# A fused mLSTM, MoE and cosine-MLP kernel: expert steps, exponentials and weight loads placed anew around the last attention chunks

## The chip, the cores and the metric

The kernel runs on one core of a Trainium2 chip. The metric is device time in microseconds (us) from one launch to its end. TensorE is called PE here, VectorE DVE, ScalarE ACT, GpSimd POOL and SyncE SP, as in the profile. Each engine works through its own instructions strictly in order, and waits on semaphores for the others.

## The reference

Three layers follow each other in float32. The first is an mLSTM over 2 batches, 8 heads, 768 positions and head size 40. The second is a mixture of 8 experts with top-2 routing, and the third is an MLP with x·cos(x) between its two products.

```
C = f_stab * C + i_stab * outer(v_t, k_t); n = f_stab * n + i_stab * k_t
y_t = sigmoid(o_t) * (C q_t) / max(|n q_t|, 1)
...
logits = x @ w_gate;  noise_scale = log1p(exp(x @ w_noise))
top2 of logits + noise_scale * noise, softmax over the two
out[mask] += top2_w[mask, k] * (relu(x[mask] @ w1[e]) @ w2[e])
...
h = x @ w_in;  out = (h * cos(h)) @ w_out
```

## The kernel before

The recurrence is computed in chunks of 128 positions, 6 for each batch, so there are 12 chunks, 0 to 11. `att_step(n)` writes the instructions of chunk n. For PE these are `mm_state(n)` (L274, the chunk's contribution to the state), the products `mm_s(n + 2)` (L256, queries by keys of the chunk after next), `mm_out(n)` (L314 and L318, four pairs of heads into one PSUM tile), the transposes `rt_a(n - 1)` (L354) and the router's product `rt_b(n - 1)` (L363). `mm_out(n)` calls `between(w)` after each of its four head pairs w, and other PE work can be put there. ACT makes the decay factors `mk_e(n + 1)` (L230, tile `get`), the exponentials of the weights `mk_w` (L210, eight instructions, tile `wt`; POOL then masks them, L217), the copy `xTt` of the transposes (L356), the copy `Lt` of the router's product (L367) and the absolute value `Abs` (L329) with which `mk_y(n)` begins. DVE adds the state (`mk_state`, L301), multiplies the weights in (`mk_p`, L264), forms the scaled queries (`mk_q`, L244, on POOL for some n) and ends `mk_y(n)` with L335, which makes the chunk's output rows `x(n)`. POOL also scales the keys (L236) and decays the state (`mk_decay`, L285).

When chunk 5 is done, the first batch can be routed. `router_a0` to `router_a4`, `router_b`, `router_b1`, `router_b2`, `router_c` and `router_d` rank its tokens; `router_c` (L511, twelve small matmuls, the index product) and `router_d` (L519, L520) give the rows that POOL then gathers (`gather`, L552, an indirect DMA into `xgt`). `router_s` (L482 to L484) prepares the second batch's offsets. `prep_slot` transposes gathered rows (L561), ACT copies them to `xh` (L563) and DVE forms the rest `xl` (L564, L566).

The experts come in ten groups of eight steps, 80 steps in all. Experts 0 and 1 form a small group for each batch, so that groups 0 and 1 (steps 0 to 15) need the first batch alone; groups 2 to 7 need both. `expert_step` first splits the weights two steps ahead (`split(k + 2)`: ACT copies to `wh`, L591, then DVE or POOL forms the rest `wl`, L593), then writes the first product (L600, eight matmuls), relu on ACT (L652) and the rest on DVE (L655), and then the second product (L605, L606, L609) of the step before it. `POOL_SPLIT` and a list of even numbers decide which splits go to DVE and which to POOL.

The order is written by hand. `at[n]`, `pre[n]`, `mid[n]` and `fill[n]` are lists of calls that `att_step(n)`, and later the loop over expert steps, writes at four places: `pre` behind `mk_e`, `mid` behind `mm_out`, `fill` behind the loads, `at` behind the whole chunk or step. Steps 0 to 3 stand in chunks 10 and 11, step 4 behind the last chunk, and the loop goes on with `K0 = 5`. SP issues all other transfers in the written order; `load_w` (L538) brings expert weights into two large buffers `wraw`. The PSUM tile `pM` exists once, `pS` three times and `pA` four times; who takes a tile waits until its last reader is done. Two places are to be followed in the code:

```
elif w == NH - 2 and n != 10:
    rt_a(n - 1, psS if n == 7 else None)
...
pre[9] = [(mk_w, (11, False))]
mid[9] = [(router_c, (0,)), (router_d, (0,)), (gather, (0, 0)), (gather, (0, 1)), (mk_m, (11, 0, 1)), (split, (0,))]
mid[10] = [(mk_y, (10,)), (rt_a, (9,)), (prep_slot, (0, 0, psA)), (prep_slot, (0, 1, psA))]
fill[10] = [(step, (0,))]
```

Of the kernel before, what the change touches and what calls it, by code (L numbers as in the profile page):

```python
# [41 lines left out]
def tile_mlstm_moe_moe2(ctx, tc, qk, kv, og, gi, gf, wcat, noise, wm1, wm2, cst, out):  # L42
# [539 lines left out]
    POOL_SPLIT = (1, 7, 9, 11, 65, 67, 75)  # L582

    def split(k):
        g, f = divmod(k, 8)
# [274 lines left out]
    def att_step(n):  # L860
# [51 lines left out]
        if n == 10:  # L912

            for p, r0, st, m in ((64, ROW0[2] + CAP2, 512, 6), (16, CAP1, 256, 2), (16, ROW1[0] + CAP1, 256, 2)):
                Y.dma_start(bass.AP(tensor=YD.tensor, offset=YD.offset + r0 * DM, ap=[[DM, p], [st * DM, m], [1, DM]]),
                            cc_[:p, None, 0:DM].to_broadcast([p, m, DM]))
# [25 lines left out]
    mid[9] = [(router_c, (0,)), (router_d, (0,)), (gather, (0, 0)), (gather, (0, 1)), (mk_m, (11, 0, 1)), (split, (0,))]
    fill[9] = [(split, (1,))]
    put(9, router_a3, 0)
    put(10, router_a4, 0)
    mid[10] = [(mk_y, (10,)), (rt_a, (9,)), (prep_slot, (0, 0, psA)), (prep_slot, (0, 1, psA))]
    fill[10] = [(step, (0,))]
    put(10, step, 1)
    mid[11] = [(mk_y, (11,)), (step, (2,))]
    put(11, step, 3)  # L950
# [19 lines left out]
    put(6, router_b, 1)  # L970
    put(7, router_b1, 1, 0)
    put(7, router_b1, 1, 1)
    put(8, router_b2, 1)
    put(9, router_p, 1)
    put(10, router_c, 1)
    put(10, router_d, 1)
    put(11, router_a3, 1)
    put(12, router_a4, 1)
# [194 lines left out]
```

## Time and profile before

| what | us |
|---|---|
| median of 3 runs | 516.35 |
| lowest and highest of them | 514.23, 517.95 |
| the profiled execution's own time | 515.04 |
| its span in the profile | 513.2 |
| PE busy in that span | 485.0 |
| DVE, ACT, POOL busy | 365.9, 326.0, 273.4 |

The span goes from the first to the last instruction; 1.84 us lie around it. PE is busy for 95% of it, so time is lost or won where PE waits. Chunks 6 to 11 and the first expert steps, which the change touches, lie between 53 and 127 us. A start and a duration of overlapping matmuls are modelled, so starts are compared with starts.

### The profile page before, as it was taken

To read this page: it belongs to the slowest core of one execution; us is meant where nothing else is said; L and a number is where in the kernel's file an instruction comes from. 1 tells how busy PE (TensorE), PEld (TensorE's weight loads), DVE (VectorE), ACT (ScalarE), POOL (GpSimd) and SP (SyncE) were. 2 spreads that over 40 slices of the span, in tenths; PEclk is the share of its full clock that TensorE was granted. 3 is DMA by queue.
4 is the path that set the end of the run, shared out by engine and by line. 5 is a ranking of instruction groups with operands and counts; after the bars stand their busy time and mean duration, and the time that the engine had idled before them with its cause. 6 is when DMAs were issued, how large, how long until landed. Compare 5 with 4: busy or idle time off the path is not lost.

```text
span 513.2 us, 9200 instructions
## 1 busy us (share of the span) xinstructions
PE 485.0 (95%) x3294; PEld 470.0 (92%) x3294; DVE 365.9 (71%) x776; ACT 326.0 (64%) x695; POOL 273.4 (53%) x234
## 2 busy tenths in 40 slices
PE   4998996999999999999999989899999999999994
PEld 3998996899999999999999988899999999999994
DVE  8875596687388777777775688698856665787772
ACT  3668865466455554555454566578877777787772
POOL 5435576476856777676867686273365347200000
PEclk9999999999999999999999999999999999999998
DMA  5778866782755646282939183220021003001001
GB/s 167 241 244 266 246 217 220 207 325 84 279 187 187 241 166 263 82 347 59 372 94 323 56 335 108 80 66 15 0 78 39 2 14 96 8 2 38 1 2 44
DMA packets 25397, 74.41 MB, mean 145 GB/s; under 512 B 3872, under 2 KB 11392, under 8 KB 25344
## 3 DMA queue, kind: packets, MB, share of 16 engines
q1 hardware_dynamic: 22752, 65.14, 36.9%
q0 software_dynamic: 2592, 8.61, 5.5%
q8 instruction: 28, 0.46, 0.4%
q14 instruction: 25, 0.20, 0.1%
HBM read 64.51 MB, written 9.22 MB: 144 GB/s over the span
## 4 chain that ended last, share of the span: by engine, by line
PE 79%; DVE 9%; ACT 6%; issue 2%; DMA 2%; SPq 0%; DVEq 0%; ACTq 0%
PE pS L600 35%; PE pA L609 11%; PE pA L606 10%; PE pA L605 10%; ACT wt L210 2%; PE pM L561 2%; PE pS L318 2%; PE pA L256 2%; PE pA L618 1%; PE pA L617 1%; DMA gb<-gd 1%; PE pM L363 1%; DVE c_t L723 1%; ACT get L230 1%; PE pS L314 1%
## 5 line engine op out<-in xcount | busy, mean ns | idle before, releaser
L593 POOL TENSOR_TENSOR wl<-wraw,wh 128x704 fp32r<-128x704 f32 x69 | 122.7, 1787 | 59.4 <-ACT wh L591 52.2
L655 DVE SCALAR_TENSOR_TENSOR hb<-pS,hb 128x384 fp32r<-128x384 f32 (+2 forms) x128 | 45.9, 390 | 45.2 <-ACT hb L652 44.6
L591 ACT ACTIVATE wh<-wraw 128x704 fp32r<-128x704 f32 x80 | 62.9, 786 | 14.2 <-PE pA L617 7.5
L600 PE MATMUL pS<-xh,wh 128*128 128x448 f32 (+1 forms) x240 | 69.5, 344 | 0.5 <-ACT xh L563 0.5
L600 PE MATMUL pS<-xh,w 128*128 128x384 f32 x288 | 66.5, 340 | 1.6 <-DVE m_t L764 1.5
L600 PE MATMUL pS<-xh,wl 128*128 128x448 f32 (+1 forms) x240 | 65.7, 328 | 0.3 <-POOL wl L593 0.3
L606 PE MATMUL pA<-wl,hb 128*128 128x320 f32 x208 | 62.1, 308 | 0.0
L605 PE MATMUL pA<-wh,hb 128*128 128x320 f32 x208 | 62.1, 308 | 0.0
L749 ACT ACTIVATE m_t<-pS,magic 128x384 f32<-128x384 f32 x64 | 37.0, 579 | 27.9 <-PE pS L600 24.7
L652 ACT ACTIVATE hb<-pS 128x448 fp32r<-128x448 f32 (+1 forms) x80 | 37.7, 471 | 26.1 <-PE pS L600 17.2
L600 PEld LDWEIGHTS pS<-xh,w 128*128 128x128 f32 x288 | 49.8, 188 | 2.9 <-DVE m_t L764 2.9
L764 DVE SCALAR_TENSOR_TENSOR m_t<-m_t,pS 128x384 f32<-128x384 f32 x64 | 35.4, 553 | 16.8 <-ACT m_t L763 14.7
L609 PE MATMUL pA<-wh,hb 128*128 128x320 f32 x208 | 44.0, 310 | 3.1 <-DVE hb L655 3.0
L600 PEld LDWEIGHTS pS<-xh,wl 128*128 128x128 f32 x240 | 42.7, 188 | 2.8 <-POOL wl L593 0.5
L750 DVE TENSOR_SCALAR m_t<-m_t 128x384 f32<-128x384 f32 x64 | 23.1, 361 | 26.6 <-ACT m_t L749 26.4
L600 PEld LDWEIGHTS pS<-xh,wh 128*128 128x128 f32 x240 | 40.4, 189 | 1.6 <-ACT xh L563 0.6
L770 POOL TENSOR_TENSOR wl<-m_t,wh 128x384 fp32r<-128x384 f32 x25 | 25.4, 1017 | 30.4 <-ACT wh L768 21.2
L600 PE MATMUL pS<-xl,wh 128*128 128x448 f32 (+1 forms) x160 | 39.6, 329 | 0.6 <-DVE xl L564 0.6
L605 PEld LDWEIGHTS pA<-wh,hb 128*128 128x128 f32 x208 | 38.7, 186 | 0.8
L606 PEld LDWEIGHTS pA<-wl,hb 128*128 128x128 f32 x208 | 38.6, 186 | 0.6
L552 POOL DMA_INDIRECT xgt<-xd,idx x28 | 34.5, 1230 | 7.0 <-issue 3.0
L751 DVE SCALAR_TENSOR_TENSOR m_t<-pS,m_t 128x384 f32<-128x384 f32 x64 | 35.7, 558 | 2.2
(198 smaller groups left out, 1239.7 us busy)
## 6 DMA issues: line engine op xcount, KB each, us to landing
wraw<-wm SPq DMA_DIRECT2D x36, 704.0 KB
raw<-wm SPq DMA_DIRECT2D x16, 704.0 KB
gb<-gd SPq DMA_DIRECT2D x10, 512.0 KB
kv<-kv SPq DMA_DIRECT2D x12, 324.0 KB
qk<-qk SPq DMA_DIRECT2D x24, 160.0 KB
yd<-yt SPq DMA_DIRECT2D x22, 160.0 KB
wraw<-wm SPq DMA_DIRECT2D x8, 352.0 KB
ogt<-og SPq DMA_DIRECT2D x6, 320.0 KB
```

Source lines behind the costliest of these rows:

```text
L552: G.indirect_dma_start(out=t[:n, :], out_offset=None, in_=XD[0:S, :] if g < 2 else XD[:, :], in_offset=bass.IndirectOffsetOnAxis(ap=(idxe ...
L591: A.activation(wh, raw[:, f, :], AF.Copy)
L593: eng.tensor_tensor(out=wl, in0=raw[:, f, :], in1=wh.bitcast(FT), op=OP.subtract)
L600: T.matmul(p[:, :n], w[:, 128 * k:128 * k + 128], x[:, m, :], start=(i == 0), stop=(i == 7))
L605: T.matmul(a[:n, :DM], hh[:, s], wh[:, KW:], start=first, stop=False)
L606: T.matmul(a[:n, :DM], hh[:, s], wl[:, KW:], start=False, stop=False)
L609: T.matmul(a[:n, :DM], hl[:, s], wh[:, KW:], start=False, stop=last)
L652: A.activation(hh[:, :n], p[:, :n], AF.Relu)
L655: V.scalar_tensor_tensor(out=hb[:, o:o + z - a], in0=p[:, a:z], scalar=0.0, in1=hh[:, a:z].bitcast(FT), op0=OP.max, op1=OP.subtract)
L749: A.activation(t, m["p"], AF.Identity, bias=magic, scale=0.5 / PI)
L751: V.scalar_tensor_tensor(out=t, in0=m["p"], scalar=0.5 / PI, in1=t, op0=OP.mult, op1=OP.subtract)
L764: V.scalar_tensor_tensor(out=s, in0=s, scalar=1.0, in1=m["p"], op0=OP.subtract, op1=OP.mult)
```

## The change

No arithmetic is added or removed. Steps 0 to 3 leave chunks 10 and 11: only step 0's first product still stands in chunk 11, behind its outputs, step 1 comes behind the last chunk, and the loop starts with `K0 = 2`. The index product, its conversion and the first two gathers move from the place behind all of chunk 9's outputs to that behind its first pair of heads. The exponentials of chunks 9 and 10 move from the ends of chunks 7 and 8 to the beginnings of chunks 7 and 8 (as those of chunk 11 already stood at the beginning of chunk 9). The ACT table load moves from the middle of chunk 6 to the end of chunk 5. `rt_a(8)` takes a `pS` tile and `rt_b(8)` the `pM` tile, `rt_a(9)` stands between the heads of chunk 10, and `mk_y(10)` behind chunk 10's fill. The splits, weight loads, the clearing of `yd`, the second batch's router and the gathers of group 2 get other steps, and four splits and one `mk_q` change their engine.

```diff
-        (G if n in (1, 4, 5, 6, 7, 8, 9, 11) else V).tensor_tensor(out=d["qt"], in0=d["qk"][:, 1], in1=d["ge"], op=OP.mult)
+        (G if n in (1, 4, 5, 6, 7, 8, 9) else V).tensor_tensor(out=d["qt"], in0=d["qk"][:, 1], in1=d["ge"], op=OP.mult)
...
-    POOL_SPLIT = (1, 7, 9, 11, 65, 67, 75)
+    POOL_SPLIT = (1, 3, 7, 65, 67, 75)
...
-            elif w == NH - 2 and n != 10:
-                rt_a(n - 1, psS if n == 7 else None)
+            elif w == NH - 2:
+                rt_a(n - 1, psS if n in (7, 9) else None)
+            if w == 0 and n == 9:
+                router_c(0)
+                router_d(0)
+                gather(0, 0)
+                gather(0, 1)
...
-        if n < 9:
+        if n < 7:
             mk_w(n + 2)
...
-        put((6, 7, 8, 8, 8, 9, 9, 9)[i], load_w, 0, i, 1)
+        put((6, 7, 7, 8, 10, 10, 10, 11)[i], load_w, 0, i, 1)
...
-    mid[6] = [(A.preload_act_table_set, ("natural_log_exp_and_others",))]
+    put(NC - 1, A.preload_act_table_set, "natural_log_exp_and_others")
...
+    pre[7] = [(mk_w, (9,))]
+    pre[8] = [(mk_w, (10,))]
...
+    fill[10] = [(split, (0,)), (split, (1,))]
+    put(10, router_a3, 0)
+    put(10, prep_slot, 0, 0, psA)
+    mid[11] = [(mk_y, (11,)), (prep_slot, (0, 1, psA))]
+    fill[11] = [(step, (0,))]
...
+        put(11, gather, 1, i)
-    K0 = 5
+    K0 = 2
...
-    step(4)
+    step(1)
```

Three places show how the engines' instructions stand. The first is ACT from the end of chunk 5 (the tanh, L158) to chunk 7, before:

```order
L158 ACTIVATE ogt<-ogt 128x640
L230 ACTIVATE get<-gb 64x512 x2
L356 ACTIVATE xTt<-pM 128x384
L881 ACT_TABLE_LOAD
L367 ACTIVATE Lt<-pM 128x16
...
L210 ACTIVATE wt<-gb,tok 128x128 x8
L230 ACTIVATE get<-gb 64x512 x2
L356 ACTIVATE xTt<-pS 128x384
L367 ACTIVATE Lt<-pM 128x16
```

The same stretch of the change:

```order
L158 ACTIVATE ogt<-ogt 128x640
L960 ACT_TABLE_LOAD
L230 ACTIVATE get<-gb 64x512 x2
L356 ACTIVATE xTt<-pM 128x384
L367 ACTIVATE Lt<-pM 128x16
...
L210 ACTIVATE wt<-gb,tok 128x128 x8
L230 ACTIVATE get<-gb 64x512 x2
L210 ACTIVATE wt<-gb,tok 128x128 x8
L356 ACTIVATE xTt<-pS 128x384
L367 ACTIVATE Lt<-pM 128x16
```

The table load now stands ahead of `mk_e(7)` and the copy `xTt(5)`, and the eight exponentials of chunk 9 ahead of the copy `xTt(6)`. The second place is PE in chunk 9, the change as a difference with its - and +. L511 is the index product, of whose twelve weight loads and matmuls the first row ends the piece; L354 are the transposes `rt_a(8)`.

```order
 L256 MATMUL pA<-qk_93 128x128 x2
-L314 MATMUL pS<-st_99,qtt 128x82
-L318 MATMUL pS<-kv,ppt 128x2x41 x2
-L256 MATMUL pA<-qk_93 128x128 x2
-L314 MATMUL pS<-st_99,qtt 128x82
-L318 MATMUL pS<-kv,ppt 128x2x41 x2
-L354 MATMUL pM<-ident,xt 128x128 x3
-L314 MATMUL pS<-st_99,qtt 128x82
-L318 MATMUL pS<-kv,ppt 128x2x41
-L318 MATMUL pS<-kv,ppt 128x82
-L256 MATMUL pA<-qk_93 128x128 x2
 L511 LDWEIGHTS r_am
```

Three pairs of heads and the transposes of chunk 8, which stood ahead of the index product, stand behind it now. The third place is ACT from the factors `mk_e(11)` in chunk 10 to the first relu, before:

```order
L230 ACTIVATE get<-gb 64x512 x2
L329 ACTIVATE pS<-pS 128x8
L356 ACTIVATE xTt<-pM 128x384
L563 ACTIVATE xh<-pA 128x3x128
L563 ACTIVATE xh<-pA 128x3x112
L367 ACTIVATE Lt<-pM 128x16
L591 ACTIVATE wh<-wraw 128x704
L652 ACTIVATE hb<-pS 128x240
```

And there in the change:

```order
L230 ACTIVATE get<-gb 64x512 x2
L356 ACTIVATE xTt<-pM 128x384
L367 ACTIVATE Lt<-pM 128x16
L591 ACTIVATE wh<-wraw 128x704 x2
L329 ACTIVATE pS<-pS 128x8
L436 ACTIVATE r_w_1147<-r_w_1147 128x6
L563 ACTIVATE xh<-pA 128x3x128
L356 ACTIVATE xTt<-pM 128x384
L329 ACTIVATE pS<-pS 128x8
L563 ACTIVATE xh<-pA 128x3x112
L367 ACTIVATE Lt<-pM 128x16
```

Two weight copies L591 stand ahead of `Abs(10)` (the first L329), and the exponential L436 of `router_a3` ahead of the copies that follow.

## Rows read from the trace of the kernel before

**Rows 1.** The page's part 1: busy us, share of the span, instructions

```profile
PE 485.0 (95%) x3294; PEld 470.0 (92%) x3294; DVE 365.9 (71%) x776; ACT 326.0 (64%) x695; POOL 273.4 (53%) x234
```

**Rows 2.** PE's timeline, chunk 6 to step 5: start, us, instruction, [idle before, releaser]

```profile
58.60 0.94 PE L363 MATMUL pM<-wc,xTt 128*128 128x128 f32 x6 [0.38 <-ACT xTt L356]
...
65.43 0.91 PE L363 MATMUL pM<-wc,xTt 128*128 128x128 f32 x6 [0.39 <-DVE r_os L429]
...
75.36 0.35 PE L314 MATMUL pS<-st,qtt 128*128 128x82 f32 x2
...
80.03 0.45 PE L511 MATMUL pM<-r_bm,r_am 128*128 128x32 f16 x12 [1.31 <-ACT xTt L356]
...
83.34 0.45 PE L314 MATMUL pS<-st,qtt 128*128 128x82 f32 x2 [0.85 <-DVE qtt L244]
...
86.09 0.49 PE L354 MATMUL pM<-ident,xt 128*128 128x128 f32 x3
...
88.72 0.94 PE L363 MATMUL pM<-wc,xTt 128*128 128x128 f32 x6 [1.53 <-ACT xTt L356]
...
90.78 0.49 PE L600 MATMUL pS<-xl,wh 128*128 128x240 f32 x2 [0.62 <-DVE xl L564]
...
93.43 0.56 PE L609 MATMUL pA<-wh,hb 128*128 128x320 f32 x2 [0.37 <-DVE hb L655]
...
101.26 0.47 PE L600 MATMUL pS<-xh,wh 128*128 128x240 f32 x2
...
103.11 0.83 PE L363 MATMUL pM<-wc,xTt 128*128 128x128 f32 x6
103.70 0.47 PE L600 MATMUL pS<-xh,wh 128*128 128x240 f32 x2
```

**Rows 3.** ACT's timeline, chunk 6 to step 5

```profile
58.05 0.49 ACT L356 ACTIVATE xTt<-pM 128x384 f32<-128x384 f32 x1
58.56 1.28 ACT L881 ACT_TABLE_LOAD   x1
...
59.86 0.18 ACT L367 ACTIVATE Lt<-pM 128x16 f32<-128x16 f32 x1
...
64.33 0.49 ACT L356 ACTIVATE xTt<-pS 128x384 f32<-128x384 f32 x1
...
77.16 2.44 ACT L210 ACTIVATE wt<-gb,tok 128x128 f32<-128x128 f32 x8
79.51 0.46 ACT L356 ACTIVATE xTt<-pM 128x384 f32<-128x384 f32 x1
79.88 0.78 ACT L591 ACTIVATE wh<-wraw 128x704 fp32r<-128x704 f32 x1
...
88.00 0.15 ACT L329 ACTIVATE pS<-pS 128x8 f32<-128x8 f32 x1
...
103.98 0.18 ACT L367 ACTIVATE Lt<-pM 128x16 f32<-128x16 f32 x1 [1.01 <-PE pM L363]
```

**Rows 4.** DVE's timeline, chunk 8 to step 12

```profile
74.72 0.56 DVE L502 TENSOR_TENSOR r_bm<-r_jm,tok_id 128x384 f16<-128x384 f32 x1
...
84.58 2.11 DVE L435 TENSOR_TENSOR r_w<-r_mx 128x6 f32<-128x6 f32 x1
...
89.17 0.49 DVE L335 SCALAR_TENSOR_TENSOR xt<-pS,ogt 128x320 f32<-128x320 f32 x1
...
118.21 0.16 DVE L435 TENSOR_TENSOR r_w<-r_mx 128x6 f32<-128x6 f32 x1
```

**Rows 5.** POOL's timeline, chunks 9 and 10

```profile
82.42 0.94 POOL L552 DMA_INDIRECT xgt<-xd,idxe  x1 [0.31 <-issue]
...
84.56 1.68 POOL L593 TENSOR_TENSOR wl<-wraw,wh 128x704 fp32r<-128x704 f32 x1
86.19 1.01 POOL L285 TENSOR_TENSOR st<-st,get 40x164 f32<-40x164 f32 x2
```

**Rows 6.** Tile xgt over the whole run: time of the gathers to landing

```profile
DMA to landing us min/median/max: 2.9/5.2/5.6
```

More of the change, by code (lines that the diff above doesn't have):

```diff
@@ L591, in split @@
         A.activation(wh, raw[:, f, :], AF.Copy)
-        eng = V if len(groups[g][1]) == 2 and (k % 2 and k not in POOL_SPLIT or k in (12, 14)) else G
+        eng = V if len(groups[g][1]) == 2 and (k % 2 and k not in POOL_SPLIT or k in (10, 12)) else G
         eng.tensor_tensor(out=wl, in0=raw[:, f, :], in1=wh.bitcast(FT), op=OP.subtract)
@@ L911, in att_step, with clear_yd @@
             gates_b(4, NC)
[L912 to L916, printed above, removed]
+    def clear_yd():
+        for p, r0, st, m in ((64, ROW0[2] + CAP2, 512, 6), (16, CAP1, 256, 2), (16, ROW1[0] + CAP1, 256, 2)):
+            Y.dma_start(bass.AP(tensor=YD.tensor, offset=YD.offset + r0 * DM, ap=[[DM, p], [st * DM, m], [1, DM]]),
+                        cc_[:p, None, 0:DM].to_broadcast([p, m, DM]))
     at, pre, mid, fill = {}, {}, {}, {}
@@ L928, in tile_mlstm_moe_moe2 @@
     for i in range(8):
-        put((6, 7, 8, 8, 8, 9, 9, 9)[i], load_w, 0, i, 1)
-    put(10, load_w, 1, 0, 2)
-    put(11, load_w, 1, 2, 2)
-    put(11, load_w, 1, 4, 2)
-    mid[6] = [(A.preload_act_table_set, ("natural_log_exp_and_others",))]
+        put((6, 7, 7, 8, 10, 10, 10, 11)[i], load_w, 0, i, 1)
+    put(11, load_w, 1, 0, 2)
+    put(NC - 1, A.preload_act_table_set, "natural_log_exp_and_others")
     fill[6] = [(router_a0, (0,))]
@@ L936, in tile_mlstm_moe_moe2 @@
     put(6, router_a2, 0)
+    pre[7] = [(mk_w, (9,))]
     fill[7] = [(router_b, (0,))]
     put(7, router_b1, 0, 0)
+    pre[8] = [(mk_w, (10,))]
     fill[8] = [(router_b1, (0, 1)), (router_b2, (0,))]
-    put(8, router_s)
     pre[9] = [(mk_w, (11, False))]
[L942 to L950, printed above, removed]
+    fill[9] = [(mk_m, (11, 0, 1))]
+    put(9, router_s)
+    fill[10] = [(split, (0,)), (split, (1,))]
[3 more added lines that the diff above has]
+    fill[11] = [(step, (0,))]
+    put(11, router_a4, 0)
     for i in range(2):
-        put(9, gather, 1, i)
-    K0 = 5
+        put(11, gather, 1, i)
+    K0 = 2
     for n in range(2 * NC):
@@ L964, in tile_mlstm_moe_moe2 @@
     wp = ctx.enter_context(tc.tile_pool(name="wp", bufs=1, reuse_waits="tile"))
-    put(5, load_w, 1, 6, 2)
-    put(5, router_a2, 1)
+    put(2, load_w, 1, 2, 2)
+    put(2, clear_yd)
+    put(3, load_w, 1, 4, 2)
+    put(4, load_w, 1, 6, 2)
+    put(3, router_a2, 1)
+    put(4, router_b, 1)
+    put(5, router_b1, 1, 0)
     put(5, prep_slot, 1, 0, psA)
+    put(6, router_b1, 1, 1)
     put(6, prep_slot, 1, 1, psA)
[L970 to L978, printed above, removed]
+    put(7, router_b2, 1)
+    put(8, router_p, 1)
+    put(8, router_c, 1)
+    put(8, router_d, 1)
+    put(10, router_a3, 1)
+    put(11, router_a4, 1)
     for i in range(4):
-        put(10 + i // 2, gather, 2, i)
+        put(8 + i // 2, gather, 2, i)
         put((13, 14, 15, 15)[i], prep_slot, 2, i, (psA, psM)[i % 2])
@@ L988, in tile_mlstm_moe_moe2 @@
         for h in range(4):
-            put(9 + 8 * i + 2 * h if i else (6, 6, 7, 7)[h], load_w, e, 2 * h, 2)
+            put(9 + 8 * i + 2 * h if i else 9 + h, load_w, e, 2 * h, 2)
     def conv_sched(f, ks):
```

4 lines of the change are left out of this document (2 added, 2 removed).

## The prediction

> **What bounds the kernel now.** I read the page's busy times first. PE is busy 485.0 us [rows 1] of a span of 513.2, and the edits leave PE's list of work as it is, so the change can only move PE's waits. The second view is PE's timeline from chunk 6 to step 5 [rows 2]: the reader is to look at the brackets, where a wait and its releaser stand. Seven rows have one, of 0.38, 0.39, 1.31, 0.85, 1.53, 0.62 and 0.37 us: 5.45 us, which is about all that can be won here. Third, for each of them, the timelines of ACT [rows 3], DVE [rows 4] and POOL [rows 5], where one sees what the late engine did instead. At 80.03 PE has no work of its own that is late: the index product needs the tile `pM`, which is free when `xTt(8)` is copied, and ACT does chunk 11's exponentials first, from 77.16 to 79.51. At 83.34 chunk 10's outputs wait for DVE, at 88.72 the router's product waits for a copy on ACT, which had waited for a DVE subtraction of six columns that took 2.11 us [rows 4]. So this stretch is bound by the chain ACT, DVE, POOL between chunks, with expert steps as filler between them.
>
> I follow one clock, the start of the same piece of PE work in both kernels, and call the difference the delay.
>
> **Chunk 6: the table load goes ahead.** ACT is at work without a gap when it copies `xTt(5)` at 58.05; right behind it comes the table load of 1.28 us, and `Lt(5)` starts at 59.86 [rows 3]. PE's router product waits for that copy [rows 2]. The load holds ACT from the copy's end, 58.54, to its own, 59.84. With it ahead of `mk_e(7)` and the copy, these come 1.30 later, and so does PE: delay +1.30. Before, the load lay beside PE's next products and cost PE nothing. A bound from below is zero, if ACT had slack there, which its gapless row speaks against. The Trainium skill (page ScalarE: Activation LUTs, section What ACT_TABLE_LOAD costs) puts the load at 1283 ns and, with a drain, every switch to another set at about 2.66 us. By that figure the estimate of this term would be 2.66, and the total 1.36 above the sum below. The trace agrees with the 1283 ns and shows no drain: the load begins 0.02 us after the copy's end, and `Lt(5)` starts 0.02 us after the load's.
>
> **Chunk 7: chunk 9's exponentials go ahead of xTt(6).** `Lt(5)` needs the router's product, 0.87 us from its start (103.11 to 103.98 [rows 2, 3]), so it starts at 59.90 + 0.87, about 60.8. From `Lt(5)` to `xTt(6)` ACT needs 4.47 us (59.86 to 64.33, no gap [rows 3]); eight exponentials are added, 2.35 (77.16 to 79.51). `xTt(6)` so starts at 67.6, ends at 68.1, and PE's product starts at 68.15 instead of 65.43 [rows 2]: delay +2.72, 1.42 of it from this step. The other waiter there, DVE's ranking, is only 0.9 later and done before. Everything of chunk 8 then runs at +2.72 without a wait, since ACT has the exponentials of chunk 9 behind it.
>
> **Chunk 9: the index product.** It now stands behind the first pair of heads, where PE begins the second pair at 75.36 [rows 2]; with the delay that is 78.1. Its last input `r_bm` ended at 75.28 [rows 4], with the delay 78.0. So it starts at once or a few tenths late; I add 0.2. `rt_a(8)` in a `pS` tile is copied before PE needs it, since chunk 11's exponentials end earlier than it starts. The waits of 1.31 and 0.85 go, and PE runs on from there: three pairs, the transposes and the router's product (0.6, 103.11 to 103.70) bring chunk 10's heads to 83.0 instead of 83.34 [rows 2]. Delay there -0.3.
>
> **Chunks 10 and 11, the filler taken out.** Heads to transposes take 2.75 (83.34 to 86.09 [rows 2]), about 0.68 a pair. `rt_a(9)` stands behind the third pair, its copy is done at 86.1, when the fourth pair ends: the wait of 1.53 goes. Then new waits come, because there is nothing left to put between:
> - `Lt(9)` is at 86.1 + 0.87 = 87.0. Two weight copies of 0.78 [rows 3] stand between it and `Abs(10)`, so that is at 88.5, and x(10) is ready 1.66 later (88.00 to the end of L335, 89.66 [rows 3, 4]), at 90.2. Chunk 11's heads start at 87.1; after three pairs, at 89.1, `rt_a(10)` waits for x(10): 1.1 us.
> - `r_w` L435 follows x(10) on DVE. It took 0.16 us at one place and 2.11 at another, where it ended at 86.69, in the middle of POOL's state decay, whose two halves follow a split of 1.68 [rows 4, 5]. So it waits for a POOL operation. Now POOL does two splits from 88.0 to 91.4, and L435 ends there, not at 90.4. I take the upper value, since the splits lie over it. Queued behind it are the exponential L436, `xh` and `xTt(10)` on ACT; `xTt(10)` ends at 92.5, PE is free at 91.55: 1.0 us.
> - `xl` of the second slot stands on DVE behind `mk_y(11)`, which needs `Abs(11)`, behind `xTt(10)`: ready at 94.65. PE has then done four of step 0's eight matmuls and waits 0.9 (before 0.62 [rows 2]).
> - Step 0's first product ends at 95.2; transposes 0.3, step 1's first product 1.0, step 0's second 0.9, router 0.6: step 2 begins at 98.0.
>
> Before, the step behind the last router product (step 5) begins at 103.70, with three more steps done; a step takes 1.85 (101.26 to 103.11 [rows 2]). 103.70 - 3 x 1.85 = 98.15. So the delay at step 2 is **-0.15**, and +0.05 with the 0.2 of chunk 9. The gains of chunks 9 and 10 pay for the losses of chunks 6, 7 and 11.
>
> **Gathers.** The decay of the state for chunk 11 waits on POOL for the landing of the first two gathers. The first starts about 79.8, the second 81.2, and landing takes 2.9 to 5.6 [rows 6]: the second lands between 84.1 and 86.8. Mask, weights and queries of chunk 11 follow it on POOL and DVE, so the heads start between 87.1 and 89.9. Up to 89.2 that is covered by the wait for x(10); beyond it costs up to 0.7. `router_s`, behind `mk_y(9)` on DVE now, lies under the same cover.
>
> **Steps 2 to 16.** The second batch's chain gets three more steps in front of step 16, but PE prepares the last slot right ahead of step 16 in both orders and waits for its copy, so nothing is won there. POOL gets split 3 and two gathers of 0.94 [rows 5] behind split 2: with splits of 1.70, split 3 is ready at 100.0, and step 3 wants it at 100.15; up to 1.0 if one of them slips. DVE takes splits 9, 10 and 11 instead, in steps 7 to 9, where its ranking is lighter. Weight loads: split 4's transfer is issued behind x(10)'s store, at about 91, and wanted at 99; each later one has as long. I cost these at zero; their cover is those 8 us. From step 16 on both orders are the same.
>
> **Sum.** 515.04 (the profiled execution) + 1.30 + 1.42 + 0.2 - 2.87 (what chunks 9 to 11 give back net) = 515.1. The profiled execution lies 1.31 below the median of the three runs, so against that: 516.35 + 0.05, **516.4 us**. Ends of the unknown costs: table term 0 to 1.30, L435 0 to 1.0, index product 0 to 0.7, gathers 0 to 0.7, POOL behind step 0 0 to 1.0. All low: 516.4 - 1.3 - 1.0 - 0.2 = 513.9; all high: 516.4 + 0.5 + 0.7 + 1.0 = 518.6.
>
> **Rivals.**
> - Gain: ACT's later copies don't reach PE, so that chunks 6 and 7 cost nothing and chunks 9 to 11 give back what I count. For it: the exponentials are only moved, and their burst in chunk 9 goes. Against it: ACT's gapless rows from 58.05 to 64.33. The time is 516.4 - 2.72 = 513.7; with none of the three waits of chunk 11 either, 510.9.
> - Slower: POOL becomes the bound behind the attention. In steps 0 to 4 it does splits 0 to 4, 1.7 each, and two gathers, and DVE's operations on SBUF and POOL's hold each other up, as L435 beside a split shows [rows 4, 5]. If split 2 slips past 97, each step from 3 to 5 waits for its `wl`, about 1 us a step: 519.4; with late gathers 520.1. It decides from the point where split 3 ends after 100.2.
> - The loads: two buffers are filled later than before, and a step that waits for one waits whole transfers. If split 4 or 5 waits, 3 to 5 us: about 520. Against it: some 8 us of lead.
> - The table load holds ACT twice as long, since ACT has to run empty first: once more 1.30, 517.7. The load's neighbours at 0.02 us speak against it [rows 3]. This is the drain of the page named above.
>
> **How the numbers follow.** Forecast (514.6 to 518.2): 0.60. Gain: 0.20, mostly 511.3 to 514.6. POOL-bound: 0.12, loads: 0.05, both 518.2 to 522. Longer load: 0.03. The range 513.0 to 519.4 leaves out about 0.09 below and 0.08 above. About 1% (5.2 us) is what a measurement of this kernel can tell from no change. Faster by more (below 511.2) is only the far end of the gain, 0.05; slower by more (above 521.5) the far end of the late transfers and POOL, 0.06; within it 0.89.
>
> **What the profile after would show.** Chunk 6: `xTt(5)` right behind `mk_e(7)` and the load, PE's bracket at the router's product about 1.7. Chunk 7: `xTt(6)` behind eight exponentials, a bracket of about 1.8. Chunk 9: no bracket at L511 over 0.5, none at L314 of chunk 10. Chunk 11: a bracket at L354 for x(10) near 1.1, one at L363 near 1.0 with L435 longer than 1 us on DVE, one at L600 near 0.9. Step 3: no bracket for `wl`. The prediction is wrong if the brackets of chunks 6 and 7 are missing (gain), or if steps 2 to 5 show waits for `wl` or a weight load (loss).

## The result, and the profile after

The changed kernel took 519.96 us (median of 21 runs, 517.49 to 523.81), the kernel before 514.87 (21 runs, 513.65 to 518.89). The ratio is 1.0095, with an interval of 1.0075 to 1.0115: 4.9 us slower, by 3.9 to 5.9. The prediction was 516.4, with a range up to 519.4. It forecast a change of +0.05 on a base of 516.35, the median of three runs; over 21 runs the kernel before is at 514.87. So the base was 1.5 too high, by chance in the direction of the result: the two times lie 3.6 apart, but the error in the change itself is 4.9. The profiled execution of the changed kernel took 517.49, the fastest of the 21, with a span of 515.7; that of the kernel before took 515.04, with a span of 513.2. So two things have to be explained: 2.5 us between two profiles, and about 2.5 more between the profile of the changed kernel and its own median.

The busy times, which answer to [rows 1]:

```profile
PE 486.9 (94%) x3294; PEld 471.9 (92%) x3294; DVE 366.2 (71%) x778; ACT 326.3 (63%) x695; POOL 270.9 (53%) x232
```

PE has the same 3294 matmuls as before, and yet 1.9 us more busy time. Work that didn't change has become slower somewhere. PE's timeline, which answers to [rows 2] (start, us, instruction, idle before and releaser):

```profile
59.29 0.94 PE L363 MATMUL pM<-wc,xTt 128*128 128x128 f32 x6 [1.44 <-ACT xTt L356]
...
67.61 0.94 PE L363 MATMUL pM<-wc,xTt 128*128 128x128 f32 x6 [1.88 <-DVE ppt L264]
...
77.57 0.45 PE L511 MATMUL pM<-r_bm,r_am 128*128 128x32 f16 x12
...
87.56 0.45 PE L314 MATMUL pS<-st,qtt 128*128 128x82 f32 x2 [0.62 <-DVE qtt L244]
...
90.03 0.52 PE L354 MATMUL pM<-ident,xt 128*128 128x128 f32 x3 [0.24 <-DVE xt L335]
...
92.12 0.94 PE L363 MATMUL pM<-wc,xTt 128*128 128x128 f32 x6 [0.65 <-ACT xTt L356]
...
94.30 0.49 PE L600 MATMUL pS<-xl,wh 128*128 128x240 f32 x2 [0.80 <-DVE xl L564]
...
97.63 0.47 PE L600 MATMUL pS<-xh,wh 128*128 128x240 f32 x2
...
111.27 0.45 PE L609 MATMUL pA<-wh,hb 128*128 128x320 f32 x2
113.61 0.46 PE L511 MATMUL pM<-r_bm,r_am 128*128 128x32 f16 x12 [1.90 <-DVE r_fl L476]
```

The reader sees the waits of chunks 6 and 7, the index product of chunk 9 without one, the waits of chunk 11 (0.62 for `qtt`, then 0.24, 0.65 and 0.80), and step 2 beginning at 97.63. All these stand in the prediction, with other sizes in chunk 11. The row of chunk 7 names DVE's `ppt`, which ends at 67.61. What the product reads is the copy `xTt`, which ends at 67.56 on ACT:

```profile
64.74 2.44 ACT L210 ACTIVATE wt<-gb,tok 128x128 f32<-128x128 f32 x8
67.09 0.47 ACT L356 ACTIVATE xTt<-pS 128x384 f32<-128x384 f32 x1
```

The last row of PE's timeline does not stand in the prediction: in step 8 the second batch's index product waits 1.90 us for the tile `pM`, whose old content `r_fl` still reads. Before, this product stood behind step 10 and had no wait:

```profile
115.85 0.47 PE L511 MATMUL pM<-r_bm,r_am 128*128 128x32 f16 x12
```

DVE's timeline of the changed kernel shows why `r_fl` is late:

```profile
109.50 0.90 DVE L593 TENSOR_TENSOR wl<-wraw,wh 128x704 fp32r<-128x704 f32 x1
110.42 0.41 DVE L655 SCALAR_TENSOR_TENSOR hb<-pS,hb 128x240 fp32r<-128x240 f32 x1
110.75 0.56 DVE L500 TENSOR_TENSOR pM<-pM,cc 128x384 f32<-128x384 f32 x1
111.34 0.56 DVE L502 TENSOR_TENSOR r_bm<-pM,tok_id 128x384 f16<-128x384 f32 x1
111.81 0.88 DVE L593 TENSOR_TENSOR wl<-wraw,wh 128x704 fp32r<-128x704 f32 x1
112.61 0.40 DVE L655 SCALAR_TENSOR_TENSOR hb<-pS,hb 128x240 fp32r<-128x240 f32 x1
112.93 0.48 DVE L630 COPY yt<-pA 112x320 f32<-112x320 f32 x1
113.33 0.16 DVE L474 TENSOR_SCALAR r_pos<-pM 128x12 uint32<-128x12 f32 x1
113.40 0.15 DVE L476 TENSOR_TENSOR r_fl<-pM,cc 128x8 f32<-128x8 f32 x1
```

No row has a bracket: DVE never waits here. Two of its rows are the splits 9 and 10 (`wl`, 0.90 and 0.88), which the change gave to DVE. (Five splits changed their engine, not four: 3 and 14 went to POOL, and 9, 10 and 11 to DVE.) They stand ahead of the ranking's last operations, and POOL has nothing to do from 109.07 to 114.79. The index product's own input `r_bm` is ready at 111.90, 1.7 us before the product starts. The windows of the same stretch (PE, PEld, DVE, ACT, POOL busy, granted clock of PE, DMA share, GB/s):

```profile
110.00:112.00 2.00, 1.72 (x14) 1.45 (x12) 1.94 (x5) 1.55 (x4) 0.00 (x0) 1.00 0.05 8
112.00:114.00 2.00, 0.39 (x13) 0.39 (x13) 1.72 (x6) 0.73 (x2) 0.00 (x0) 1.00 0.24 81
114.00:116.00 2.00, 2.00 (x14) 2.00 (x11) 1.17 (x3) 0.29 (x1) 1.21 (x1) 0.56 0.76 186
116.00:118.00 2.00, 2.00 (x11) 2.00 (x11) 0.41 (x1) 0.71 (x2) 1.39 (x3) 0.58 0.95 352
118.00:120.00 2.00, 2.00 (x18) 2.00 (x18) 1.29 (x3) 1.01 (x4) 1.56 (x2) 1.00 1.04 430
```

Right behind the wait the granted clock goes from 1.00 to 0.50 (2.4 to 1.2 GHz) for 3.4 us, with PE busy throughout. At half clock, 3.4 us do the work of 1.7: that is most of PE's additional busy time of 1.9. Everything behind is later by the wait and by this stretch.

### The profile page after: what moved, and what is told of

Same layout as the page of the kernel before. It is cut to its first block, busy times and chain, and to the rows that moved or that the text cites. A ratio compares the mean times of both kernels' runs of the same rounds, so it can differ in the third digit from the quotient of the medians.

```text
span 515.7 us, 9208 instructions
## 1 busy us (share of the span) xinstructions
PE 486.9 (94%) x3294; PEld 471.9 (92%) x3294; DVE 366.2 (71%) x778; ACT 326.3 (63%) x695; POOL 270.9 (53%) x232
## 4 chain that ended last, share of the span: by engine, by line
PE 75%; DVE 7%; ACT 2%; issue 2%; POOL 1%; DVEq 0%; ACTq 0%; POOLq 0%
PE pS L600 35%; PE pA L609 10%; PE pA L606 10%; PE pA L605 10%; PE pM L561 2%; PE pA L618 1%; PE pA L617 1%; PE pS L318 1%; DVE c_t L723 1%; PE pA L256 1%; PE pM L363 1%; ACT xh L563 1%; DVE m_t L764 1%; DVE c_t L727 1%; DVE wl L593 0%
## 5 line engine op out<-in xcount | busy, mean ns | idle before, releaser
L593 POOL TENSOR_TENSOR wl<-wraw,wh 128x704 fp32r<-128x704 f32 x68 | 121.0, 1790 | 61.6 <-ACT wh L591 52.5
L591 ACT ACTIVATE wh<-wraw 128x704 fp32r<-128x704 f32 x80 | 62.8, 786 | 15.3 <-PE pA L617 9.1
L600 PE MATMUL pS<-xh,wh 128*128 128x448 f32 (+1 forms) x240 | 69.8, 345 | 0.5 <-ACT xh L563 0.5
L600 PE MATMUL pS<-xh,w 128*128 128x384 f32 x288 | 66.5, 340 | 1.6 <-DVE m_t L764 1.5
L600 PE MATMUL pS<-xh,wl 128*128 128x448 f32 (+1 forms) x240 | 66.3, 330 | 0.4 <-POOL wl L593 0.4
L600 PEld LDWEIGHTS pS<-xh,w 128*128 128x128 f32 x288 | 49.8, 188 | 2.9 <-DVE m_t L764 2.9
L609 PE MATMUL pA<-wh,hb 128*128 128x320 f32 x208 | 44.1, 311 | 2.8 <-DVE hb L655 2.6
L600 PEld LDWEIGHTS pS<-xh,wl 128*128 128x128 f32 x240 | 43.1, 190 | 3.1 <-POOL wl L593 0.8
L600 PEld LDWEIGHTS pS<-xh,wh 128*128 128x128 f32 x240 | 40.9, 190 | 1.6 <-ACT xh L563 0.6
L600 PE MATMUL pS<-xl,wh 128*128 128x448 f32 (+1 forms) x160 | 39.8, 330 | 0.8 <-DVE xl L564 0.8
```

Of the source, the lines that this page charges most:

```text
L600: T.matmul(p[:, :n], w[:, 128 * k:128 * k + 128], x[:, m, :], start=(i == 0), stop=(i == 7))
L609: T.matmul(a[:n, :DM], hl[:, s], wh[:, KW:], start=False, stop=last)
```

## More profiles, and a table of them

The theory after the first profile: the loss is the wait of step 8, and the stretches at half clock that follow it and the waits of chunks 6 and 7 in some executions. Its rival: each wait costs its own length and no more, and what else differs between executions is something else. A profile is one execution. Three more of the changed kernel and one of the kernel before were taken, with no edit.

> The changed kernel as it is, a second profile, to see whether the places at which the granted clock falls are the same in every execution. By the clock theory (a wait of PE of 1.4 us or more is followed by a stretch at half clock in some executions and not in others) the instructions are the same but the stretches are not: a fall is to be expected behind the L511 wait of step 8 (1.9 us, about +1.6), and now also one in chunk 6 or 7, where the first profile had waits of 1.44 and 1.88 us at clock 1.00; span 515.7 to 519. By the rival, that the loss is waits alone, the profile repeats the first: span 515.7, clock below 1.00 only at 114 to 118.

> The changed kernel once more, a third profile. Two profiles had the same waits (1.9 us in chunk 7, 1.9 us at step 8) but one stretch at half clock each: behind step 8 in the first (span 515.7), behind chunk 7 in the second (517.8). If the clock falls behind each of these waits by chance, this profile has one or both (about 1.5 us for step 8, 3.0 for chunk 7), and its span is 514.2 + 0.7 for the start + the falls: 516 to 519.5. If the spread of the times has another cause, a span of 517 or more comes with the clock at 1.00 throughout.

> The changed kernel, a fourth profile, with the same expectation as the third: the span follows the half-clock stretches behind the waits of chunk 7 (3.0) and step 8 (1.5); or, by the rival, it varies with the clock at 1.00.

> The kernel before, a second profile: by the clock theory it has no half-clock stretch between chunk 6 and step 16, since its longest wait there is 1.5 us and has filler work around it; span 513 to 514. If such stretches are there as often as in the changed kernel, the clock doesn't tell the two kernels apart.

The spans were 517.8, 515.5 and 514.8 (times 519.53, 517.20, 516.52), and 513.0 for the kernel before (514.85). The second profile of the changed kernel has the same wait in chunk 7 as the first, and the same in step 8:

```profile
68.51 0.94 PE L363 MATMUL pM<-wc,xTt 128*128 128x128 f32 x6 [1.87 <-DVE ppt L264]
...
72.72 1.06 PE L318 MATMUL pS<-kv,ppt 128*128 128x82 f32 x4
...
76.63 0.61 PE L318 MATMUL pS<-kv,ppt 128*128 128x82 f32 x4
...
117.54 0.46 PE L511 MATMUL pM<-r_bm,r_am 128*128 128x32 f16 x12 [1.89 <-DVE r_fl L476]
```

but its clock falls at the other place, behind chunk 7, and not behind step 8:

```profile
68.00:70.00 2.00, 1.22 (x15) 1.05 (x15) 0.51 (x1) 0.97 (x5) 1.85 (x3) 0.85 0.00 0
70.00:72.00 2.00, 2.00 (x17) 2.00 (x14) 1.56 (x10) 1.96 (x6) 1.62 (x4) 0.50 0.29 94
72.00:74.00 2.00, 2.00 (x11) 2.00 (x11) 1.93 (x5) 1.35 (x5) 1.22 (x2) 0.50 0.83 284
74.00:76.00 2.00, 2.00 (x12) 2.00 (x11) 1.94 (x6) 0.00 (x0) 1.75 (x2) 0.50 0.99 228
...
118.00:120.00 2.00, 2.00 (x18) 2.00 (x18) 1.58 (x4) 0.41 (x2) 1.28 (x1) 1.00 0.81 167
```

The same four score matmuls (L318) take 1.06 us at half clock and 0.61 at full. In the third and fourth profile it falls behind the wait of chunk 6 (1.79 us there), in the third behind step 8 too. For these two 516 to 519.5 had been expected, with falls behind chunk 7 or step 8; they lie below, since the fall behind chunk 6 costs little. The expectation for the kernel before failed as well: its second profile has a stretch of 3.4 us too, behind the wait of 1.53 in chunk 11 [rows 2]:

```profile
87.66 0.94 PE L363 MATMUL pM<-wc,xTt 128*128 128x128 f32 x6 [1.53 <-ACT xTt L356]
...
90.00:92.00 2.00, 2.00 (x10) 2.00 (x11) 1.94 (x5) 1.04 (x2) 1.98 (x3) 0.50 0.87 237
```

All profiles of this case together (18, with those of the sections below) show one regularity. Seven have a wait of 1.78 or 1.79 in chunk 6, and a stretch at half clock follows it each time. Two, the first and second of the changed kernel, have 1.44 and 1.00 there, since PE had lost 0.3 and 0.8 earlier in that chunk, and none follows. Where it falls in chunk 6, the wait of chunk 7 shrinks to 0.2 to 0.8 (none in one version), and the clock doesn't fall there.

Executions also differ ahead of the change: the router's product of chunk 5 starts between 51.7 and 53.2 (54.9 twice). The table therefore counts from that row, by PE's timeline: to the router's products of chunks 7 and 11 (in kernels that have three more steps ahead of the latter, less 3 x 1.85 as in the prediction), to the first transposes of the slots for step 16 (L561), and to the end of the span.

| profile | stretches at half clock, chunk 6 to step 16 | chunk 7 | chunk 11 | slot of step 16 | end |
|---|---|---|---|---|---|
| before | none | 12.66 | 44.79 | 68.81 | 460.4 |
| before, second | chunk 11 | 12.66 | 45.47 | 69.48 | 461.3 |
| changed | step 8 | 15.55 | 44.99 | 72.39 | 463.6 |
| changed, second | chunk 7 | 15.55 | 48.04 | 73.93 | 464.8 |
| changed, third | chunk 6, step 8 | 15.55 | 45.32 | 72.70 | 463.7 |
| changed, fourth | chunk 6 | 16.09 | 45.79 | 71.71 | 463.0 |
| index product in `pA` | chunk 6 | 15.54 | 45.25 | 70.12 | 461.1 |
| both moves back | step 8 | 12.66 | 43.36 | 70.78 | 461.7 |
| both, `pA` | chunk 11 | 12.66 | 44.94 | 69.77 | 460.7 |
| both, `pA`, Abs first | none | 12.66 | 42.47 | 67.47 | 458.8 |
| filler in chunks 6 and 7 | step 8 | 15.55 | 45.23 | 72.75 | 464.3 |
| filler, `pA` | none | 15.56 | 44.99 | 69.91 | 463.3 |
| before, with both moves | chunk 6 | 15.55 | 47.72 | 71.71 | 462.5 |

From chunk 11 to step 16 the first and third profile need 27.40 and 27.38, the second and fourth, with the clock at 1.00 behind the same wait, 25.89 and 25.92, and the kernel before 24.02 and 24.01. So the stretch at half clock behind step 8 is worth 1.5. The versions below that keep the wait agree: 27.40 to 27.52 in three profiles with the stretch, 25.91 in one without. That makes a fall behind this wait in five of eight profiles. Behind chunk 7 a stretch is worth 3.0 (48.04 against 44.99, a single profile, with 6.8 us at half clock). Behind chunk 6 it costs 0 to 0.5, since ACT decides when chunk 7's product can start, and PE's slower work fits into that wait. By the rival expectation the profile would have repeated itself; it didn't, and each profile's place follows its stretches to a few tenths.

## Step 8: three ways to take the wait out

Moving only the index product to another tile, so that `r_fl` and `r_pos` no longer hold it:

```
 def router_c(b):
-    p = psM()
+    p = (psA if b else psM)()
```

> The changed kernel, with the second batch's index product written to a pA tile instead of the pM tile, whose last reader is r_fl. It then waits for r_bm alone (ended at 111.9 in the trace of the change), so about 0.3 us after PE is free instead of 1.9. DVE theory: 1.5 us of the wait go; whether the clock falls after so short a wait decides the rest: span about 514 if it still falls, 512.6 if not; median 516 to 518.

518.11 us against 515.13, ratio 1.0066 (1.0041 to 1.0091), span 513.3. Its row at step 8:

```profile
112.36 0.47 PE L511 MATMUL pA<-r_bm,r_am 128*128 128x32 f16 x12 [0.23 <-DVE r_bm L502]
```

The wait is 0.23, the clock stays at 1.00, and the slot of step 16 comes 2.3 earlier than in the first profile (70.12 against 72.39).

Giving splits 9 and 10 back to POOL:

```
-POOL_SPLIT = (1, 3, 7, 65, 67, 75)
+POOL_SPLIT = (1, 3, 7, 9, 65, 67, 75)
-... or k in (10, 12)) else G
+... or k in (12,)) else G
```

> The changed kernel, with splits 9 and 10 (the rest wl) on POOL instead of DVE, everything else where the change puts it. DVE theory: DVE gets back 1.8 us before the index product of step 8, which then waits 0 to 0.3 us; no half clock; span about 512.5, median about 516. If instead the number of steps between the last router product and the index product were too few for the chain of small operations itself, the wait would stay above 1 us and the median near 519. If POOL can't take them (rival of the prediction), step 9 or 10 shows a wait for wl.

518.41, ratio 1.0058 (1.0032 to 1.0084), span 513.7; the wait is 0.73 and no half-clock stretch follows it. So 1.2 of the 1.9 us come from the two splits on DVE.

Moving the ranking's end and the index product one to two steps back:

```
-put(8, router_p, 1)
-put(8, router_c, 1)
-put(8, router_d, 1)
+put(9, router_p, 1)
+put(10, router_c, 1)
+put(10, router_d, 1)
...
-put(8 + i // 2, gather, 2, i)
+put(10 + i // 2, gather, 2, i)
```

> The changed kernel with one part undone: the second batch's router_p is written in step 9, its index product in step 10 and the gathers of group 2 in steps 10 and 11, as before the change, so that DVE has two more steps for the ranking. DVE theory (the change puts the ranking and the splits 9, 10, 11 into the same steps 5 to 8, DVE falls behind, PE waits 1.9 us for r_fl at the index product of step 8, and its clock then falls to half): no wait over 0.3 us at L511, clock 1.00 between 105 and 130 us, span about 512.3 (515.7 less 1.9 and less 1.5 for the half clock), median about 516 or lower. Rival (the loss in the median, 5 us, is larger than the 2.5 of the two profiled spans, so it comes mostly from something that the profiled run doesn't show, in chunks 6 to 11 or in transfers): span as here, but a median still above 518.

518.67, ratio 1.0072 (1.0025 to 1.0118), span 513.9. The index product waits for nothing, but the gathers, two steps later, are late:

```profile
122.68 0.55 PE L561 MATMUL pA<-ident,xgt 128*128 128x128 f32 x3 [1.46 <-DMA xgt<-xd,idx]
```

One wait is exchanged for another. The splits are still on DVE here, and the wait at the index product is gone all the same. Before, `router_p`, which forms `r_fl`, stood behind step 9 and the index product behind step 10; the change put both behind step 8. That close order alone leaves the 0.73, and the splits make 1.9 of it. In the profiles these three versions are near the kernel before (513.3 to 513.9 against 513.2). By the ratios they are 3.0 to 3.7 behind it, and the median of about 516 that was expected came in none of them; the rival expectation, a median above 518 all the same, held in all three. So something that these profiles don't show costs about 3 us, and it is still there when the wait of step 8 is gone.

## Chunks 6 and 7: the two moves on ACT

Both moves undone in the changed kernel, then each alone, then both moves alone made on the kernel before:

```
-put(NC - 1, A.preload_act_table_set, "natural_log_exp_and_others")
+mid[6] = [(A.preload_act_table_set, ("natural_log_exp_and_others",))]
...
-if n < 7:
+if n < 8:
     mk_w(n + 2)
-pre[7] = [(mk_w, (9,))]
```

> The changed kernel with two parts undone: the ACT table load back in the middle of chunk 6, and chunk 9's exponentials back at the end of chunk 7 (those of chunk 10 stay early). The prediction's terms of chunks 6 and 7 (1.30 and 1.42): the waits at the router's product of chunks 6 and 7 fall from 1.44 and 1.88 to about 0.4 each; chunk 9 then loses some of it again, since its index product would come before r_bm: 1.5 to 2.5 us less, median 517.5 to 518.5; the wait at step 8's L511 and the half clock stay. If the loss of the change sat in chunks 6 and 7, the median would fall to 515 to 516.

516.18, ratio 1.0033 (0.9999 to 1.0068). That is 3.2 us less than the changed kernel by the ratios (1 to 5 with both intervals) and 3.8 by the medians, more than expected, although step 8 still has its 1.89 us wait and a half-clock stretch in this profile.

> The changed kernel with the table load alone back in chunk 6's middle. The wait in chunk 6 goes back to about 0.4; chunk 9's exponentials still stand ahead of xTt(6), so the wait in chunk 7 is 2.3 to 3 us (1.88 plus what chunk 6 no longer takes up). By the clock theory the fall behind chunk 7 stays, and the median with it: 518.5 to 520. If the table load is what costs: 517.

> The changed kernel with chunk 9's exponentials alone back at the end of chunk 7. The wait of chunk 6 stays at 1.4 to 1.8 us, that of chunk 7 goes back to 0.4. By the clock theory a stretch at half clock still follows chunk 6 in some executions, but now nothing waits for ACT in chunk 7, so that it is no longer hidden there: 517 to 518.5. If only the exponentials cost: 516.2, as with both back.

518.63 with the table load back alone (1.0059, 1.0036 to 1.0083), 518.42 with the exponentials back alone (1.0063, 1.0039 to 1.0086). Each gives back 1.7 to 1.9 us by the ratios, to about 1.6 either way. The profile of the first has a wait of 2.16 in chunk 7 with a stretch at half clock from 69 to 76, that of the second a wait of 1.78 in chunk 6 and stretches behind it and behind step 8. One wait left is enough for a fall.

> The kernel before, with only two parts of the change: the table load ahead of chunk 6's copy xTt(5), and chunk 9's exponentials ahead of xTt(6) in chunk 7. By the prediction's own terms +2.7 at chunk 8, of which the wait of 1.31 at the index product of chunk 9 and the exponentials' burst may give back up to 1.3: 516.5 to 517.8 against 515.1. If the waits of chunks 6 and 7 bring the granted clock down in some executions, the median lies a further 1.5 to 2 above the profiled run: 518 to 519. If both moves are hidden, 515.1.

518.64, ratio 1.0077 (1.0053 to 1.0101). The two moves alone, on the kernel before, cost 4.0 by the ratio (2.7 to 5.2), almost as much as the whole change. The rows of this kernel that answer to the first two of [rows 2]:

```profile
58.97 0.94 PE L363 MATMUL pM<-wc,xTt 128*128 128x128 f32 x6 [1.79 <-ACT xTt L356]
...
67.28 0.94 PE L363 MATMUL pM<-wc,xTt 128*128 128x128 f32 x6 [0.24 <-ACT xTt L356]
```

Here the first wait's stretch at half clock has filled the second. The product of chunk 7 is 15.55 from the start row, as in the changed kernel, and the 2.9 that it is late there (15.55 against 12.66) remain at chunk 11 (47.72 against 44.79) and at step 16 (71.71 against 68.81). So 2.9 of the 4.0 are the length of the waits, and the rest is within the interval.

## Is it the clock or the waits' length? PE kept busy while it waits

The last score product of chunks 6 and 7 is computed three more times, with the same result in the same place. The copy that PE waits for comes no sooner.

```
 mm_s(n + 2, (3,) if n else range(NH))
+for _ in range({6: 3, 7: 3}.get(n, 0)):
+    mm_s(n + 2, (3,))
```

> The changed kernel with the last score product of chunks 6 and 7 repeated three times on PE (the same numbers written again, 6 matmuls of 128x128, about 0.5 us a pair), right ahead of the router's product that waits for the copy xTt. PE has work in these waits; the copy does not come sooner. By the clock theory no stretch at half clock follows in chunks 6 to 8, and the median comes down towards the profiled time of the changed kernel, 517.5, from 520.0. By the rival (what the waits cost is their own length, and something else makes the other executions longer) nothing changes: 520.0, or longer by up to 0.3 where the filler ends after the copy.

518.41, ratio 1.0072 (1.0049 to 1.0096), span 517.0. PE's rows:

```profile
57.47 1.99 PE L256 MATMUL pA<-qk 128*128 128x128 f32 x16
59.90 0.94 PE L363 MATMUL pM<-wc,xTt 128*128 128x128 f32 x6 [0.45 <-ACT xTt L356]
...
65.70 1.99 PE L256 MATMUL pA<-qk 128*128 128x128 f32 x16
68.22 0.94 PE L363 MATMUL pM<-wc,xTt 128*128 128x128 f32 x6 [0.54 <-ACT xTt L356]
```

The filler shortens the idle time to 0.45 and 0.54, the products start where they did (15.55 at chunk 7), and the clock stays at 1.00 in chunks 6 to 8. With more work on PE the ratio is 1.2 us lower and the median 1.6. That is less than the 2.5 that the clock theory gave, and with both intervals the 1.2 can be anything from -0.4 to 2.8, so the zero of the rival is not excluded.

> The changed kernel with PE's waits in chunks 6 and 7 filled (the last score product of these chunks three more times, the same numbers), and with the index product of batch 1 in a pA tile, so that the wait behind r_fl at step 8 goes too. The table load and chunk 9's exponentials stay where the change put them, so that the copies and all that follows come as late as in the changed kernel. By the clock theory the waits' own length in chunks 6 and 7 costs little in the end, and the half-clock stretches behind them cost the rest: median within 1 us of its profiled run, at 515 to 516, 2 to 3 below the same kernel without filler (518.1). By the rival (the lateness of the copies is what costs): 518 as without filler.

> The version with filler in chunks 6 and 7 and the index product in a pA tile, a second profile. Its first had the clock at 1.00 throughout and still a span of 516.5, with 0.4 at the start, 0.6 for a gather at 172 and 0.8 at 302 to 311. If these are chance, this one is at 513.5 to 515; if they belong to the version, it repeats 516 to 517.

Filler and the `pA` tile together: 517.39, ratio 1.0028 (1.0005 to 1.0051), against 1.0066 without the filler. Eleven of its twelve runs have a mean granted clock of 0.994 to 0.999 and one is at 0.989, where the changed kernel's median is 0.989 and that of the kernel before 0.991 to 0.993. The falls behind chunks 6 and 7 are gone from all three profiles with filler, and the ratio is 2.0 us lower than without it, to 1.7 either way. The profiles show no such gain: the slot of step 16 comes at 69.91 and 70.23, and at 70.12 without filler and with a stretch behind chunk 6. And 515 to 516 was expected; 1.4 us remain over the kernel before, whose clock is lower. The second profile was not at 513.5 to 515 either: span 517.0 (518.70), of which 2.2 are lost ahead of chunk 5, with a stretch at half clock at 43 to 47 where neither version was edited.

## A version that is faster than both

Both moves back and the index product in a `pA` tile:

> Both undone together: the router's index product of batch 1 in a pA tile (no wait behind r_fl at step 8), the table load back to chunk 6's middle and chunk 9's exponentials back to the end of chunk 7 (no waits of 1.4 and 1.9 us in chunks 6 and 7); only the reordering of chunks 9 to 11 and of the splits is left. If the three waits are the whole loss: span about 513.3 - 1.7 = 511.6 to 512.5, time 513.5 to 514.3, below the kernel before by 0.8 to 1.5 us, and a median within 1 us of the profiled execution. If the two parts overlap, or if the steps of group 0 have a loss of their own: 515 to 516.

514.44 against 514.90, ratio 0.9997 (0.9974 to 1.0020): no difference that can be told, and less than expected. What is left of the change is the order of chunks 9 to 11, of the splits and of the weight loads. So the loss of the whole change sits, to about 1.2 us, in the two moves on ACT and in the wait of step 8; the later weight loads have no large part in it. In that version's chunk 10, ACT copies the weights of splits 0 and 1 (1.47 us) before `Abs(10)`. The last edit puts them behind it:

```
-fill[10] = [(split, (0,)), (split, (1,))]
+put(10, split, 0)
+put(10, split, 1)
 put(10, router_a3, 0)
```

> The version with both parts undone (514.4 against 514.9 of before), and the two weight copies of splits 0 and 1 behind chunk 10's Abs on ACT instead of ahead of it. Abs(10) then starts at Lt(10)'s end, 85.9 instead of 87.3 in that version's trace, x(10) ends 1.4 earlier, and the six-column subtraction L435 ends ahead of POOL's splits. The waits at L354 (0.29), L363 (0.64) and part of that at L600 (0.81) go: 1.0 to 1.5 less, median 513.0 to 513.5. If splits 0 and 1, then 0.2 to 0.4 later, make step 0 wait for its weights, or if the subtraction meets POOL again: 514.4.

513.64 against 515.35, ratio 0.9970 (0.9944 to 0.9996), span 510.9, the clock at 1.00 up to step 16: faster than both kernels by a little. DVE's six-column subtraction and POOL's pair of splits beside it, in the version without this edit:

```profile
86.80 3.32 POOL L593 TENSOR_TENSOR wl<-wraw,wh 128x704 fp32r<-128x704 f32 x2 [1.60 <-ACT wh L591]
...
88.88 1.26 DVE L435 TENSOR_TENSOR r_w<-r_mx 128x6 f32<-128x6 f32 x1
```

and with it:

```profile
86.33 3.34 POOL L593 TENSOR_TENSOR wl<-wraw,wh 128x704 fp32r<-128x704 f32 x2 [1.17 <-ACT wh L591]
...
87.79 0.27 DVE L435 TENSOR_TENSOR r_w<-r_mx 128x6 f32<-128x6 f32 x1
```

It had been expected ahead of the splits. It came behind the first one's start, but before its end (half of 3.34 past 86.33 is 88.0), and in both kernels it ends where a split ends, at 88.06 and 90.14. So it waited for the end of the first split here, and of the second there. The waits at L354 and L363 of chunk 11 are gone as expected, that of L600 is 0.57 instead of 0.81, and a wait for `qtt` ahead of chunk 11's heads has grown from 0.57 to 1.19.

## Why the prediction was wrong

**What held.** The chain of chunks 6 to 11 came out as written in its first half, and in its sum. Chunk 6: +1.30 predicted, and the row is 1.40 later (7.23 from the start row against 5.83). Chunk 7: +2.72 predicted, +2.89 measured (15.55 against 12.66), with brackets of 1.44 and 1.88 for the 1.7 and 1.8 foretold. The index product of chunk 9 has no wait. In chunk 11 the waits foretold as 1.1, 1.0 and 0.9 are 0.24, 0.65 and 0.80. Counted from the start row, x(10) was ready 0.4 later than foretold (37.83 against 37.43), but the heads of chunk 11 began 1.2 later (35.50 against 34.33), 0.62 of it the wait for `qtt` that the paragraph on the gathers allows for, so that less was left to wait for x(10). L435 took 1.26 beside POOL's splits. Step 2 was put at a delay of +0.05, and chunk 11's product is at 44.99 against 44.79. ACT's timeline has the table load without a gap:

```profile
56.16 1.28 ACT L960 ACT_TABLE_LOAD   x1
57.45 1.27 ACT L230 ACTIVATE get<-gb 64x512 f32<-64x512 f32 x2
58.74 0.49 ACT L356 ACTIVATE xTt<-pM 128x384 f32<-128x384 f32 x1
```

The load takes ACT 1.28 us and no more, so the rival of a longer load falls. The Trainium skill (page ScalarE: Activation LUTs, section What ACT_TABLE_LOAD costs) has a drain in the price of a switch; this trace shows 1.28 us and 0.01 to the next operation, and no drain.

**The step that failed: steps 2 to 16 at zero.** The prediction counted 8 us of cover there, for the transfers, and no wait of PE. It said that DVE takes splits 9, 10 and 11 "in steps 7 to 9, where its ranking is lighter". It is not lighter: DVE is busy for 1.94 of the 2.00 us from 110 to 112, the ranking's last operations and the index product are in step 8, the order on DVE has splits 9 and 10 ahead of them, and the change left no step between the last reader of `pM` and the product that takes it next. The rows of before had no wait there, and it was taken for slack that would stay. Neither of the two signs of being wrong that the prediction named came, since the wait lies behind the steps 2 to 5 that it told the reader to watch. Measured from chunk 11 to step 16: +3.4 in the first profile (27.40 against 24.02). The wait is 1.9 of it (25.9 in the second and fourth profile), the half clock behind it 1.5. In the `pA` version +0.85 remain (24.87), 0.5 of it a wait for `hb` at L609 in a later step.

**A term that was missing: the clock.** Each wait in the sum had the price of its own length, and the prediction looked at the granted clock nowhere. In some profiles 3.4 or 6.8 us at half clock followed the waits of chunks 6 and 7 and of step 8. The profiles price such a stretch at 1.5 behind step 8, at 3.0 behind chunk 7 and at 0 to 0.5 behind chunk 6. How much of the loss in the median comes from them is not shown. Undoing the two moves was worth some 3.2 us, where the table gives them 1.6 in length (43.36 against 44.99 at chunk 11), but the interval of the 3.2 takes in the 1.6. And the kernel before has such stretches too, behind its 1.53 [rows 2] for one.

**The rivals.** The slower one had nearly the measured time, 519.4, for a reason that isn't there, so its nearness is luck: one weight load on PE in step 3 waits 0.2 us for POOL's split, no other step from 2 to 8 does, and POOL is idle at step 8. No step waits for a transfer of weights. The gain didn't come, since ACT's copies do reach PE. (Its far end was summed as 510.9; 513.7 less 1.1, 1.0 and 0.9 is 510.7.)

**From the profile to the median.** From the start row to the end the first profile of the changed kernel is 3.2 us longer than that of the kernel before (463.6 against 460.4), and this is the part that the rows account for. By the ratios the kernels stand above the kernel before by 4.9 (changed), 3.4 (index product in `pA`), 1.4 (filler too), -0.2 (moves back instead of filler) and -1.5 (Abs first), each to about 1.2 either way. Read as steps: 1.5 for step 8, 2.0 for the filler, 1.6 for the lateness of ACT's copies. The single steps are no surer than 1.7, their sum is. In the 21 runs of the changed kernel the time follows the mean granted clock: the eight runs at 0.992 or more have a median of 518.9, the six below 0.988 one of 522.3. But the clock doesn't tell the two kernels apart: of 69 runs of the kernel before, 35 are at 0.992 or more, and their median is 514.7, so that at a like clock the changed kernel is still 4.2 us slower. **Open** is therefore what the 1.7 us are by which the executions differ more than the two first profiles (4.9 less 3.2), and why the four profiled executions (516.5 to 519.5) are mostly better than the others, also at the same clock (517.49 and 516.52 at 0.995, where a run without a trace took 519.46): the others have no trace, so what they wait for and where their clock fell isn't shown. Open too are the 1.4 us that the filler version with the `pA` tile keeps although its clock is high; 1.6 for lateness would account for them, but its two profiles have other losses in them as well.

## What to carry to other kernels

Price a new wait of the engine that sets the end by its length and by what the granted clock may do behind it, and look at the windows' clock column beside every bracket over a microsecond. When work is given to another engine, read what stands in that engine's queue right behind the place and who waits for it, also through a buffer that is merely read. One profile is one execution: when its time is at the edge of the runs, take another before explaining the difference. Take the base of a forecast from more than three runs.

## What the hardware did that was not expected

- The granted clock fell to 0.50 behind waits of 1.78 to 2.16 us in chunks 6 and 7, of 1.9 in step 8 and of 1.53 in chunk 11 of the kernel before, and stayed there for 3.4 us, or 6.8 in the two falls of chunk 7, with PE busy throughout. Behind the same waits in other executions it stayed at 1.00: in three of eight profiles behind step 8, and in one behind chunk 7 (1.88). The same four matmuls (L318) took 1.06 us instead of 0.61.
- A stretch at half clock cost nothing in chunk 6 in most profiles (15.55 at chunk 7 with it and without; 16.09 in one), where another engine decided when PE could go on, and 3.0 in chunk 7.
- DVE's subtraction of six columns took 0.16 us where POOL was not in its way and 2.11 where it was [rows 4], and in three later traces it ended to 0.1 us where a split of POOL ended (in the changed kernel at 91.06, POOL's pair at 91.04).
